# Aligned pairs of PSUM banks, v in even and odd halves, and new orders, in an attention kernel with a maxout layer

## The chip, the cores and the metric

The kernel runs on one core of a Trainium2 chip. The core has a matrix engine (TensorE, PE in the profile), three engines for everything else (VectorE or DVE, ScalarE or ACT, GpSimd or POOL), a queue for transfers (SyncE, SP) and 16 DMA engines. Matrix products land in PSUM, which the kernel uses as eight banks of 512 float32 values per partition; operands lie in SBUF. The engines run beside each other, each through its own instructions in order, and wait for each other by semaphores. The metric is the device time of one execution in microseconds (us), lower is better; the median of several runs is compared.

## The reference

Block-sparse attention with a local window, then a maxout layer with an output projection:

```python
B, H, S, D = q.shape                       # 4, 8, 768, 64
block, window = (32, 16); nb = S // block  # 24 blocks
k_sum = k.reshape(B, H, nb, block, D).max(axis=3)
v_sum = v.reshape(B, H, nb, block, D).mean(axis=3)
scores_l = scale * np.matmul(q, k.transpose(0, 1, 3, 2))
mask_l = np.abs(pos[:, None] - pos[None, :]) < window
scores_s = scale * np.einsum('bhsd,bhnd->bhsn', q, k_sum) + np.log(block)
scores_l_m = np.where(mask_l, scores_l, -1000000000.0)
a = softmax(np.concatenate([scores_l_m, scores_s], axis=-1))
attn = np.matmul(a, np.concatenate([v, v_sum], axis=2))
x = attn.transpose(0, 2, 1, 3).reshape(B * S, H * D)   # 3072 x 512
h1 = x @ w1                                # 512 x 1024
h2 = x @ w2
out = np.maximum(h1, h2) @ w_out           # 1024 x 512
```

Every query sees at most 31 neighbouring keys and the 24 block maxima of its head.

## The kernel before

**Stages.** For each batch b and pair of heads hp (four pairs) `prep` (lines 499 to 569) casts k and q to bf16, transposes them (by TensorE, for six late pairs by a DMA) and builds a key tile `kx`: for every 64 queries 128 columns, namely 64 main keys, 32 neighbours ("tails") and 32 columns for block maxima ("sums"). The maxima come from a reduction on DVE (L546). `cast_v` and `spread_v` (lines 389 to 482) build the value tile `vx` in the same manner. Its original shape is 12 tiles of 64 positions by 8 heads by 66 columns (64 values and ones), with even and odd position tiles alternating in memory. The even tiles are cast from the landed v; odd tiles are copied from them over partitions ("odd v"); block means are made by six matmuls (L459), copied out of PSUM to a tile `sums`, and spread to every position tile ("all sums"). In batch 0 this goes by single pairs of heads, with the block means in tiles of their own (`apart`); in batches 1 to 3 one call does all eight heads.

**Attention.** A batch has three groups (grp) of 256 positions. For each group and two pairs of heads: `scores` (L591) fills one bank per pair of heads; `weigh` takes the exponential of both banks in one ScalarE operation (L603) and multiplies by a 0/1 mask on DVE (L611; in batch 0 the mask is added on TensorE instead, L581); `values` (L641, L645) fills two more banks with weighted values and row sums; DVE inverts the row sums (L657) and scales both banks in one operation (L660) to `xs`, which is transposed to `xt` by a DMA in batches 1 to 3.

**Maxout.** max(h1, h2) is computed as h1 + relu(h2 - h1). The differences w2 - w1 are the tile `wd`, and w1 @ w_out is multiplied out once (`make_w1o`, L732). For each group, `maxout` makes four hidden tiles (L749) with a relu each (L759 on ACT, L761 on DVE), and `out_part` adds x @ (w1 @ w_out) (L777) and relu @ w_out (L784) in one bank, copies it out and stores it.

**What sets the order.** The kernel issues nothing directly. Every step is handed to `plan.op` with its planned duration on each engine that may do it, its buffers and a priority. `Plan.run` (lines 155 to 205) then plays the engines forward in time and always takes the ready step of lowest priority number; the resulting sequence is what each engine gets. Priorities and engines come from two long constants, CFG["prios"] (one number per step) and CFG["engines"] (one letter per step: D, A, P, T, S). Buffers are slots of rings (`Ring`, `Buf`): a step can start only when all slots that it needs are free. The eight PSUM banks are one ring, with limits per kind: 2 for key/query transposes, 4 for scores, 3 for values, 3 for hidden and output (`"mm": 2 + CFG["relu"]`), none for the rest. A wide operation reads its two banks, whichever they are, by one access with a step:

```python
in_=spread(bank_tile[:, pss[0].ap, 0:1], [512 * (pss[1].ap - pss[0].ap), 2], [128, 4], [64, 2], [1, 64]),
...
step = lambda: 512 * (pss[1].ap - pss[0].ap)
```

The semaphores themselves are not written in the kernel: the framework derives them from what each operation reads and writes, in the planned sequence. Small copies of all kinds go through one helper, so that they carry line 492 in the profile; they are told apart by tile and shape.

Of the kernel before, what the change touches and what calls it, by code (L numbers as in the profile page):

```python
# [14 lines left out]
F32 = mybir.dt.float32  # L15
BF16 = mybir.dt.bfloat16
# [10 lines left out]
    woc=600, wdp=30, lk="ADDP", lq="AAPA", lod="DPS", lse="DDD", lsr="DDS", lvc="DPPPDDAPPAPA", ltl="DDPD", ld=500, relu=1, warm=(), cold=12500,  # L27
# [31 lines left out]
""".split()))  # L59
CFG["engines"] = "".join("""  # L60
DPDAADPDDPPDPDPDDADPDDDPPPPSSSDPPPTDDSSSPAPDTDDSSSADPATDDSSSPPPATDASSDATASSPATASSPPTDSSDATDSPSPSASPPTATDDPAPDDDTATDD
PDAADATPTDDADPDDPTPTDDAAPADTTATTDDTATTATTDDTDTTATTDDTDTTATTDDTATTATTDDTATTATTDDTDSSSPSSSASSSASSSDPDADPTADDDDDTPTADPD
PDAATPTDDPPAADTTADTTDDSTTADTTDDSTTADTTDDSDTATADADPAAPTATADDDDDATTADTTDDSTTADTTDDSTTADTTDDSSSSDSSSPSSSASSSPPPPDPTDDDD
PDTPTADAPAAAATPTDDDAAADTTADTTDDSTTADTTDDSTTADTTDDSDSASADPDDDDPSDSADDPPADTTADTTDDSTTADTTDDSTTADTTDDSSSSDSSSDSSSDSSSDP
ADPATDSPDPASDSADDAAPAASASADAPPAATTADTTDDSTTADTTDDSTTADTTDDSDSASDDPAPAPDSASADDPAPDTTADTTDDSTTADTTDDSTTADTTDDSTTATTATT
DTTDTATDTATDTTTDSTTTDSTATDTDTATTTASTTTASTDTATDTATTTASTTTASTATATDTATTTDSTTTASTATATDTDTTTASTTTDSTDTATATDTTTDSTTTASTDTD
TATDTTTASTTTDSTDTATATDTTTASTTTDSTATDTATDTTTASTTTDSTDTDTATATTTDSTTTASTATATDTDTTTASTTTASTATDTATDTTTDSTTTDSTTTDATTTDS
# [4 lines left out]
class Ring:  # L72


    def __init__(self, slots, cap=None):
        self.slots, self.cap = slots, cap or {}
        self.owner = [None] * len(slots)

    def find(self, buf, now):
        ends = [-1 if o is None else o.end() for o in self.owner]  # L80
        if buf.kind in self.cap and self.cap[buf.kind] <= sum(
                o is not None and o.kind == buf.kind and end > now for o, end in zip(self.owner, ends)):
            return None
        return min((s for s, end in enumerate(ends) if end <= now), default=None, key=lambda s: (ends[s], s))


class Buf:
# [11 lines left out]
    def take(self, slot):  # L99
        self.slot, self.ring.owner[slot] = slot, self  # L100

# [107 lines left out]
def kernel(  # L209
# [39 lines left out]
    def bank(buf, n=512, dt=F32):  # L249
        a = bank_tile[:, buf.ap]  # L250
        return (a if dt is F32 else a.bitcast(BF16))[:, 0:n]
# [12 lines left out]
    vxr = Ring(tiles("vx", 2, [128, NT, H, VW], BF16))  # L264
    stg = Ring(tiles("sums", 1, [128, H, VW], BF16))
# [30 lines left out]
    def fixed_parts():  # L296
# [5 lines left out]
        def ones(e, t):  # L302
            on(e).memset(t[:, :, :, D:VW], 1.0)
# [40 lines left out]
        for hs in (slice(0, 4), slice(4, 8)):  # L344
            op("A", {"P": 0.9, "D": 0.85, "A": 0.87}, lambda e, hs=hs: zero(e, by_parity(0)[32:64, 1, :, hs]),
               write=[vx[0], apart_in], prio=0.15, label="gap")
# [29 lines left out]
        op("P", 1.0, lambda e: make_hide(), write=[half[0]], prio=-9, label="hide")  # L376
        for n in range(2):
            op("D", {"D": 0.08, "P": 0.13}, lambda e, n=n: hide_odd(e, 64 * n), read=[half[0]], write=[half[1 + n]],
               prio=-8, port=True, label="hide odd")
        op("D", {"D": 0.08, "P": 0.18}, lambda e: hide_last(e), read=half[:3], write=[half[3]], prio=-8, port=True,  # L380
           label="hide last")
        op("D", {"D": 0.13, "P": 0.2}, lambda e: hide_wrap(e), read=half[3:], write=[hide_in], prio=-8, label="hide wrap")
        op("D", {"D": 0.4, "P": 0.7}, lambda e: on(e).memset(amean[:], 0.0), write=[amean_in], prio=-2, label="amean")
        op("D", {"D": 0.28, "P": 0.45}, lambda e: ones_amean(e), change=[amean_in], prio=0.2, label="amean")
# [28 lines left out]
    def by_parity(b):  # L413
        return vx[b].ap[:].rearrange("p (m w) h c -> p w m h c", w=2)

# [3 lines left out]
    def cast_v(b, hp, engine, prio):  # L419
# [4 lines left out]
            by_parity(b)[:, 0, :, 2 * hp:2 * hp + 2, 0:D].rearrange("p m h d -> p h m d"),  # L424
# [3 lines left out]
    def spread_v(b, h0, h1, prio, engines):  # L428

        n, hs = h1 - h0, slice(h0, h1)  # L430
        src = [mains[b, hp] for hp in range(h0 // 2, h1 // 2)]
        out = [vx[b], *(ready[b, hp] for hp in range(h0 // 2, h1 // 2))]
        took, ps, st = Buf(Ring([None])), Buf(banks, "mm"), Buf(stg)
        tag, whole = f"{b}{h0}", n == H
        s_rows = slice(96, 128)
        if whole:
            fresh = Buf(Ring([None]))
            op("P", 0.2, lambda e: nc.gpsimd.memset(by_parity(b)[s_rows, 0, :, :, D:VW], 1.0),
               read=[mains[b, 0]], write=[vx[b], fresh], prio=prio, label=f"ones {b}")
            src = [*src, fresh]  # L440
# [130 lines left out]
    def scores(b, hp, grp, prio, mask_on):  # L571
# [3 lines left out]
        def view():  # L575
            return bank(ps).rearrange("p (i a w q) -> p i a w q", i=2, a=2, w=2)
# [311 lines left out]
```

## Time and profile before

| what | value |
|---|---|
| median of 3 runs | 194.22 us (194.13 to 196.07) |
| profiled execution | 192.87 us |
| its span, first to last instruction | 191.1 us |
| granted TensorE clock | 1.0 throughout |
| HBM read, written | 25.17 MB, 6.29 MB |
| TensorE weight loads, by the page | 113.2 us |

A row of the page for a group of instructions has the line, engine, operation, what is written from what is read, shapes and count; then the busy time and the mean duration in ns; then the idle time of that engine just before these instructions, and which instruction ended most of it. "PE banks L777 <- ACT pb L603" in the list of waits reads: TensorE, about to run line 777, sat idle until the ScalarE instruction of line 603 ended. Matmuls are pipelined, so the duration of a single one is longer than its share of a running queue.

### The profile page before, as it was taken

The page shows a single profiled execution, that of the slowest core. Times are in us where ns is not written, and L with a number is a line of the kernel's source. Part 1 is how long each engine was busy: PE and PEld are TensorE (multiplying, and loading weights), DVE is VectorE, ACT ScalarE, POOL GpSimd, SP SyncE. Part 2 cuts the span into 40 slices and gives each one's busy share as a digit, 9 for nine tenths or more (in the row PEclk, how much of TensorE's full clock was granted, in tenths as well). Part 3 has the DMA queues.
Part 4 walks back from the last instruction along what each step waited for, and adds up shares of the span by engine and source line. Part 5 has one row for each costly group of instructions (what it writes and reads, how often), then busy time and mean ns, then how long its engine had stood idle before and what let it go on. Part 6 is the DMA issues. An engine that isn't in the chain of part 4 may idle for free.

```text
span 191.1 us, 4050 instructions
## 1 busy us (share of the span) xinstructions
PE 163.3 (85%) x1598; PEld 113.2 (59%) x1598; DVE 117.6 (62%) x236; ACT 104.5 (55%) x143; POOL 57.6 (30%) x86
## 2 busy tenths in 40 slices
PE   0589785999977988899679976999999979998993
PEld 0369785766834654658456643585675547676553
DVE  5988554767974895677676454874778446241212
ACT  8486657765877395475776305756477244223020
POOL 7968689261601210780200002007164000000000
PEclk9999999999999999999999999999999999999999
DMA  6999999999995699349886976987651423134033
GB/s 189 365 261 272 331 370 363 376 365 296 256 245 202 177 230 144 99 70 190 192 230 174 240 189 160 197 209 165 205 135 28 137 42 127 28 95 73 0 110 111
DMA packets 69858, 36.53 MB, mean 191 GB/s; under 512 B 54640, under 2 KB 65872, under 8 KB 69840
## 3 DMA queue, kind: packets, MB, share of 16 engines
q1 hardware_dynamic: 69696, 36.22, 73.8%
q8 instruction: 12, 0.20, 0.5%
q10 hardware_dynamic: 144, 0.07, 0.1%
q14 instruction: 6, 0.05, 0.1%
HBM read 25.17 MB, written 6.29 MB: 165 GB/s over the span
## 4 chain that ended last, share of the span: by engine, by line
PE 69%; DVE 11%; ACT 9%; DMA 6%; issue 2%; SPq 1%; POOL 1%; DVEq 0%; ACTq 0%; POOLq 0%
PE banks L784 19%; PE banks L749 17%; ACT pb L603 9%; PE banks L777 8%; PE banks L591 6%; PE banks L641 6%; DVE vx L492 4%; DVE xs L660 4%; DMA land<-in_q_dram 4%; PE banks L732 4%; PE banks L520 2%; PE banks L459 2%; DMA xt<-xs 2%; PE banks L581 2%; SPq L399 1%
## 5 line engine op out<-in xcount | busy, mean ns | idle before, releaser
L749 PE MATMUL banks<-xt,wd 128*128 128x256 bf16 x384 | 47.0, 272 | 3.0 <-DVE xs L660 1.8
L784 PE MATMUL banks<-wo,g 128*128 128x512 bf16 (+2 forms) x208 | 47.0, 362 | 2.0 <-ACT pb L603 1.1
L749 PEld LDWEIGHTS <-wd 128*128 128x128 bf16 x384 | 36.8, 98 | 11.7 <-issue 3.1
L603 ACT ACTIVATE pb<-banks 128x1024 bf16<-128x1024 f32 x24 | 24.3, 1022 | 26.5 <-PE banks L591 10.0
L784 PEld LDWEIGHTS <-g 128*128 128x128 bf16 x208 | 18.7, 97 | 19.2 <-issue 2.5
L759 ACT ACTIVATE g<-banks 128x512 bf16<-128x512 f32 x24 | 14.3, 598 | 25.0 <-PE banks L749 20.9
L777 PE MATMUL banks<-w1o,xt 128*128 128x512 bf16 (+2 forms) x104 | 24.2, 362 | 2.5 <-ACT pb L603 1.4
L761 DVE TENSOR_SCALAR g<-banks 128x512 bf16<-128x512 f32 x24 | 16.5, 689 | 15.4 <-PE banks L749 12.5
L641 PE MATMUL banks<-vx,pb 128*128 128x65 bf16 (+1 forms) x384 | 19.6, 193 | 3.3 <-ACT pb L603 2.3
L641 PEld LDWEIGHTS <-pb 128*128 128x128 bf16 (+1 forms) x384 | 17.9, 97 | 6.6 <-issue 4.4
L591 PE MATMUL banks<-qx,kx 128*128 128x128 bf16 (+2 forms) x208 | 17.5, 219 | 2.6 <-ACT pb L603 1.7
L591 PEld LDWEIGHTS <-kx 128*128 128x128 bf16 x208 | 14.9, 100 | 7.5 <-issue 3.6
L657 DVE RECIPROCAL inv<-banks 128x8 f32<-128x8 f32 x24 | 5.0, 207 | 22.7 <-PE banks L641 7.3
L660 DVE TENSOR_TENSOR xs<-banks,inv 128x512 bf16<-128x512 f32 x24 | 16.6, 691 | 3.7 <-PE banks L749 2.6
L520 PE MATMUL banks<-ident,kqb 128*128 128x128 f32 x60 | 11.9, 323 | 7.8 <-ACT kqb L492 5.4
L611 DVE TENSOR_TENSOR pb<-pb,mask 128x256 bf16<-128x256 bf16 (+1 forms) x36 | 13.9, 428 | 5.6 <-ACT pb L603 5.6
L492 ACT COPY o<-banks 128x512 f32<-128x512 f32 x13 | 7.6, 586 | 17.3 <-PE banks L784 17.3
L492 DVE COPY o<-banks 128x512 f32<-128x512 f32 (+2 forms) x13 | 7.9, 609 | 13.3 <-PE banks L784 13.1
L777 PEld LDWEIGHTS <-xt 128*128 128x128 bf16 x104 | 9.4, 97 | 11.2 <-issue 1.9
L492 POOL CAST kqb<-land 128x768 bf16<-128x768 f32 x10 | 11.3, 1141 | 14.7 <-ACT vx L492 8.4
L546 DVE TENSOR_REDUCE ks<-kx 128x24 bf16<-128x768 bf16 x16 | 15.1, 945 | 0.2
L492 POOL COPY vx<-vx 32x640 bf16<-32x640 bf16 (+5 forms) x12 | 11.7, 973 | 9.7 <-ACT vx L492 8.2
(85 smaller groups left out, 206.8 us busy)
## 6 DMA issues: line engine op xcount, KB each, us to landing
land<-in_q_dram SPq DMA_DIRECT2D x16, 384.0 KB, 6.6
land<-in_k_dram SPq DMA_DIRECT2D x16, 384.0 KB, 5.3
land<-in_v_dram SPq DMA_DIRECT2D x16, 384.0 KB, 5.8
out_dram<-o SPq DMA_DIRECT2D x19, 256.0 KB, 2.3
land<-in_moe_w_dram SPq DMA_DIRECT2D x8, 512.0 KB, 7.9
land<-in_moe_w_out_dram SPq DMA_DIRECT2D x4, 512.0 KB, 9.7
out_dram<-o SPq DMA_DIRECT2D x4, 224.0 KB, 2.5
xt<-xs SPq DMA_TRANSPOSE x18, 2.5
```

The lines of the kernel that those rows point to most:

```text
L492: {"D": nc.vector.tensor_copy, "A": nc.scalar.copy, "P": nc.gpsimd.tensor_copy}[e](out=o, in_=i)
L520: nc.tensor.transpose(out=bank(ps)[:, 128 * j:128 * j + 128], in_=src.ap[:].bitcast(F32)[:, 128 * j:128 * j + 128], identity=ident32[:])
L546: op("D", 0.95, lambda e: nc.vector.tensor_reduce(out=ks.ap[:, 0:nb], in_=free(kt(), 128, [256, NM], [192, 2], [32, 2], [1, 32]), axis=AX. ...
L591: nc.tensor.matmul(out=view()[:, i // 2, :, i % 2, n0:n1], lhsT=w, rhs=qx[b, hp].ap[:, :, c:c + n1 - n0], start=(mask_on != "T"), stop=(ma ...
L603: op("A", {"A": 1.06}, lambda e: nc.scalar.activation(out=spread(pb.ap[:, :, :, 0:128], [4 * 192, 2], [192, 4], [128, 2], [1, 64]), in_=sp ...
L641: nc.tensor.matmul(out=av(n)[:, u, a, :], lhsT=p[r], rhs=vx[b].ap[r, 4 * grp + 2 * u + par, h, 0:D + 1], start=(par == 0), stop=(b > 0 and ...
L660: op("D", 0.7, lambda e: nc.vector.tensor_tensor(out=x.ap[:].rearrange("p n u a d -> p n (u a) d"), in0=spread(bank_tile[:, pss[0].ap, 0:1 ...
L749: nc.tensor.matmul(out=bank(ps)[:, 256 * s:256 * s + 256], lhsT=wd[n].ap[:, c, 128 * s:128 * s + 128], rhs=x.ap[:, c, :], start=(c == 0), ...
L759: nc.scalar.activation(out=o, in_=i, func=ACT.Relu)
L761: nc.vector.tensor_scalar_max(out=o, in0=i, scalar1=0.0)
L777: nc.tensor.matmul(out=bank(ps, c1 - c0), lhsT=x.ap[:, c, sl], rhs=w1o[c].ap[:, cols], start=(c == 0), stop=False)
L784: nc.tensor.matmul(out=bank(ps, c1 - c0), lhsT=g.ap[:, f, sl], rhs=wo[f // 2].ap[:, f % 2, cols], start=False, stop=(f == FC - 1))
```

## The change

Five edits go together.

1. Rings learn a kind that takes two aligned neighbours (a negative limit). A score group and a value group each take one such pair; at most two pairs of each kind are held. Single buffers prefer a bank whose partner is taken. The limit for hidden and output is 4. `CFG["relu"]` (1 before, which made groups of one) is gone; the relu works on one bank as before.

```diff
+        self.two = {k for k, n in self.cap.items() if n < 0}
...
+        if buf.kind in self.two:
+            ends = [max(ends[s], ends[s + 1]) if s % 2 == 0 else now + 1 for s in range(len(ends))]
+            return min((s for s, end in enumerate(ends) if end <= now), default=None, key=lambda s: (ends[s], s))
+        return min((s for s, end in enumerate(ends) if end <= now), default=None,
+                   key=lambda s: (ends[s ^ 1] <= now, ends[s], s) if self.two else (ends[s], s))
...
-    banks = Ring(list(range(8)), {"kq": 2, "sc": 4, "av": 3, "mm": 2 + CFG["relu"]})
+    banks = Ring(list(range(8)), {"kq": 2, "sc": -2, "av": -2, "mm": 4})
...
-            in_=spread(bank_tile[:, pss[0].ap, 0:1], [512 * (pss[1].ap - pss[0].ap), 2], [128, 4], [64, 2], [1, 64]),
+            in_=spread(bank_tile[:, ps.ap, 0:1], [128, 8], [64, 2], [1, 64]),
...
-            in0=spread(bank_tile[:, pss[0].ap, 0:1], [step(), 2], [D + 1, 4], [1, D]),
+            in0=spread(bank_tile[:, ps.ap, 0:1], [512, 2], [D + 1, 4], [1, D]),
```

2. The value tile has its even and odd position tiles in halves of their own, and within a half the pairs of heads one after the other, so that a copy of several pairs of heads is one long run.

```diff
-    vxr = Ring(tiles("vx", 2, [128, NT, H, VW], BF16))
-    stg = Ring(tiles("sums", 1, [128, H, VW], BF16))
+    vxr = Ring(tiles("vx", 2, [128, 2, NP, NM, 2, VW], BF16))
+    stg = Ring(tiles("sums", 2, [128, H // 2, VW], BF16))
```

3. In batches 1 to 3 `spread_v` is called twice, for two pairs of heads each. A call has one memset of ones, three odd copies (four before, per batch), the block means as six matmuls of 256 columns (512 before), one copy to `sums`, and two spreads (four before, per batch). In these batches the third odd copy comes after the second.

```diff
-        spread_v(b, 0, H, at + 11, (CFG["lod"][b - 1], CFG["lse"][b - 1], CFG["lsr"][b - 1]))
+        for g in (0, 2):
+            spread_v(b, g, g + 2, at + 11 + g, (CFG["lod"][b - 1], CFG["lse"][b - 1], CFG["lsr"][b - 1]))
```

4. In `prep` the tails also wait for the block maxima's reduction, and the spread of the maxima waits for the tails.

```diff
-           read=[kmain, kwrap], write=[kx[b, hp]], prio=prio, label=f"tails k{tag}")
+           read=[kmain, kwrap, ks], write=[kx[b, hp], tailed], prio=prio, label=f"tails k{tag}")
...
-             read=[ks], write=[kx[b, hp]], prio=prio, label=f"sums k{tag}")
+             read=[ks, tailed], write=[kx[b, hp]], prio=prio, label=f"sums k{tag}")
```

5. CFG["prios"] and CFG["engines"] are replaced as a whole (825 steps, 810 before), and a dozen planned durations are altered, such as 1.06 to 1.03 for the exponential, 1.0 to 1.65 for the making of `hide` and 0.49 to 0.51 for the values of batch 0. The durations and priorities act through the sequence alone. By the letters, the four spreads of the block means in batch 1 go from four on DVE to two on DVE, one on ACT and one on POOL; in batches 2 and 3 one odd copy each goes by SP's queue, in place of one spread in batch 3; and the four casts of q in batch 0 go from two on ACT and two on POOL to four on POOL.

More of the change, by code (lines that the diff above doesn't have):

```diff
@@ L77, in __init__ @@
         self.owner = [None] * len(slots)
+        self.two = {k for k, n in self.cap.items() if n < 0}
     def find(self, buf, now):
         ends = [-1 if o is None else o.end() for o in self.owner]
-        if buf.kind in self.cap and self.cap[buf.kind] <= sum(
-                o is not None and o.kind == buf.kind and end > now for o, end in zip(self.owner, ends)):
-            return None
-        return min((s for s, end in enumerate(ends) if end <= now), default=None, key=lambda s: (ends[s], s))
+        if buf.kind in self.cap and abs(self.cap[buf.kind]) <= len({
+                o for o, end in zip(self.owner, ends) if o is not None and o.kind == buf.kind and end > now}):
+            return None
+        if buf.kind in self.two:
[3 more added lines that the diff above has]
+                   key=lambda s: (ends[s ^ 1] <= now, ends[s], s) if self.two else (ends[s], s))
 class Buf:
@@ L100, in take @@
         self.slot, self.ring.owner[slot] = slot, self
+        if self.kind in self.ring.two:
+            self.ring.owner[slot + 1] = self
     @property
@@ L423, in cast_v, with spread_v @@
         copy(engine, {"D": 0.57, "A": 0.84, "P": 0.83}, lambda: (
-            by_parity(b)[:, 0, :, 2 * hp:2 * hp + 2, 0:D].rearrange("p m h d -> p h m d"),
+            vx[b].ap[:, 0, hp, :, :, 0:D].rearrange("p m h d -> p h m d"),
             landed(f, 2, NM * D).rearrange("p h (m d) -> p h m d", d=D)),
              read=[f], write=[vx[b], done, ready[b, hp]], prio=prio, label=f"cast v{b}{hp}")
[L428 to L434, printed above, removed]
+    def spread_v(b, g0, g1, prio, engines):
+        n, late = 2 * (g1 - g0), b > 0
+        hs, gs = slice(2 * g0, 2 * g1), slice(g0, g1)
+        src = [mains[b, hp] for hp in range(g0, g1)]
+        out = [vx[b], *(ready[b, hp] for hp in range(g0, g1))]
+        took, ps = Buf(Ring([None])), Buf(banks, "mm")
+        tag = f"{b}{2 * g0}"
@@ L435, in spread_v @@
         s_rows = slice(96, 128)
-        if whole:
+        if late:
             fresh = Buf(Ring([None]))
-            op("P", 0.2, lambda e: nc.gpsimd.memset(by_parity(b)[s_rows, 0, :, :, D:VW], 1.0),
-               read=[mains[b, 0]], write=[vx[b], fresh], prio=prio, label=f"ones {b}")
+            op("P", {"P": 0.16, "D": 0.14}, lambda e: on(e).memset(vx[b].ap[s_rows, 0, gs].rearrange(
+                "p g m a c -> p (g m a) c")[:, :, D:VW], 1.0),
+               read=src, write=[vx[b], fresh], prio=prio, label=f"ones {b}")
@@ L440, in spread_v, with runs @@
             src = [*src, fresh]
-        def odd(lo, hi, ms, shift):
-            w, ds = by_parity(b), slice(0, VW if whole else D)
-            return (w[lo:hi, 1, ms, hs, ds],
-                    w[lo:hi, 0, slice((ms.start + shift) % NM, (ms.stop + shift - 1) % NM + 1), hs, ds])
-        parts = ((0, NM // 2), (NM // 2, NM)) if whole else ((0, NM),)
-        for i, (lo, hi, ms, shift) in enumerate((
-                *((64, 128, slice(*m), 0) for m in parts), (0, 32, slice(0, NM - 1), 1), (0, 32, slice(NM - 1, NM), 1))):
-            cols = (ms.stop - ms.start) * n * D
-            copy(engines[0], {"D": 0.12 + cols * 0.0003, "P": 0.06 + cols * 0.00095, "A": 0.2 + cols * 0.00083,
-                              **({"S": 1.0 if lo else 0.83 if i == 2 else 0.2} if whole else {})},
-                 lambda lo=lo, hi=hi, ms=ms, shift=shift: odd(lo, hi, ms, shift),
-                 read=src, write=[*out, took], prio=prio, label=f"odd v{tag}{i}")
+        def runs(r, w, m0, m1):
+            t = vx[b].ap[r, w, gs, m0:m1]
+            if late:
+                return t.rearrange("p g m a c -> p g m (a c)")
+            return t.rearrange("p g m a c -> p (g m a) c")[:, :, 0:D]
@@ new lines, in spread_v @@
+        before = []
+        for i, (r, m0, m1, shift) in enumerate((
+                (slice(64, 128), 0, NM, 0), (slice(0, 32), 0, NM - 1, 1), (slice(0, 32), NM - 1, NM, 1 - NM))):
+            cols, done = (m1 - m0) * n * D, Buf(Ring([None]))
+            copy(engines[0], {"D": 0.12 + cols * 0.00032, "P": 0.06 + cols * 0.00095, "A": 0.2 + cols * 0.00083,
+                              **({"S": (1.05, 0.46, 0.12)[i]} if late else {})},
+                 lambda r=r, m0=m0, m1=m1, shift=shift: (runs(r, 1, m0, m1), runs(r, 0, m0 + shift, m1 + shift)),
+                 read=[*src, *before], write=[*out, took, done], prio=prio, label=f"odd v{tag}{i}")
+            before = [done] if i == 1 and late else []
@@ L456, in sums @@
         def sums():
-            w = by_parity(b)
             for m in range(NM):
-                nc.tensor.matmul(out=bank(ps, n * D), lhsT=amean[:, m, :], rhs=w[:, 0, m, hs, 0:D],
+                nc.tensor.matmul(out=bank(ps, n * D), lhsT=amean[:, m, :], rhs=vx[b].ap[:, 0, gs, m, :, 0:D],
                                  start=(m == 0), stop=(m == NM - 1))
@@ L469, in spread_v @@
             return
+        st = Buf(stg)
         copy(engines[1], {"D": 0.12 + n * D * 0.0011, "A": 0.18 + n * D * 0.00083}, lambda: (
-            st.ap[:, hs, 0:D], bank(ps, n * D).rearrange("p (h d) -> p h d", d=D)),
+            st.ap[:, :, 0:D], summed()),
              read=[ps, blocks_in], write=[st], prio=prio, port=False, label=f"sums {tag}")
-        for i, (w, r, ms) in enumerate((w, r, m) for w, r in ((0, s_rows), (1, slice(32, 64))) for m in parts):
-            cols = (ms[1] - ms[0]) * n * VW
-            def aps(w=w, r=r, ms=ms):
-                return (by_parity(b)[r, w, slice(*ms), hs, :],
-                        st.ap[r, hs, :].rearrange("p h d -> p (h d)").rearrange(
-                            "p (o h d) -> p o h d", o=1, d=VW).to_broadcast([32, ms[1] - ms[0], n, VW]))
-            copy(engines[2], {"D": 0.07 + cols * 0.00029, "P": 0.1 + cols * 0.00086,
-                              "A": 0.2 + cols * 0.00083, "S": 0.5}, aps,
-                 read=[st, *([took] if w == 0 else [])], write=out, prio=prio, label=f"all sums {tag}{i}")
+        cols = NM * n * VW
@@ new lines, in spread_v, with aps @@
+        for w, r in ((0, s_rows), (1, slice(32, 64))):
+            def aps(w=w, r=r):
+                a = st.ap[r]
+                return (vx[b].ap[r, w, gs].rearrange("p g m a c -> p g m (a c)"),
+                        spread(a, [2 * VW, g1 - g0], [0, NM], [1, 2 * VW]))
+            copy(engines[2], {"D": 0.12 + cols * 0.00034, "P": 0.1 + cols * 0.00088,
+                              "A": 0.2 + cols * 0.00083}, aps,
+                 read=[st, *([took] if w == 0 else [])], write=out, prio=prio, label=f"all sums {tag}{w}")
@@ L628, in values @@
     def values(b, hp, grp, pb, prio, xt_on="D"):
-        pss, tag = [Buf(banks, "av") for _ in range(2)], f"{b}{hp}{grp}"
+        ps, tag = Buf(banks, "av"), f"{b}{hp}{grp}"
         def av(n):
-            return bank(pss[n])[:, 0:4 * (D + 1)].rearrange("p (u a d) -> p u a d", u=2, a=2)
+            return bank(ps, second=n)[:, 0:4 * (D + 1)].rearrange("p (u a d) -> p u a d", u=2, a=2)
         def mm(n):
@@ L741, in maxout, with hid, relu @@
         x, g = xt[b, grp], Buf(gr)
[L742 to L757 removed]
+        for n in range(4):
+            ps = Buf(banks, "mm")
+            def hid(n=n, ps=ps):
+                for s in range(2):
+                    for c in range(KC):
+                        nc.tensor.matmul(out=bank(ps)[:, 256 * s:256 * s + 256],
+                                         lhsT=wd[n].ap[:, c, 128 * s:128 * s + 128],
+                                         rhs=x.ap[:, c, :], start=(c == 0), stop=(c == KC - 1))
+            op("T", 0.87, lambda e, hid=hid: hid(), read=[x, wd[n]], write=[ps], prio=prio, label=f"hidden {b}{grp}{n}")
+            def relu(e, n=n, ps=ps):
+                o = g.ap[:, 2 * n:2 * n + 2, :].rearrange("p f n -> p (f n)")
                 if e == "A":
[L759 removed]
+                    nc.scalar.activation(out=o, in_=bank(ps), func=ACT.Relu)
                 else:
[L761 to L763 removed]
+                    nc.vector.tensor_scalar_max(out=o, in0=bank(ps), scalar1=0.0)
+            op("A", {"A": 0.6, "D": 0.69}, relu, read=[ps], write=[g], prio=-1, label=f"relu {b}{grp}{n}")
         last = b == B - 1 and grp == NG - 1
@@ L806, in attention @@
             for grp in range(NG):
-                pss = [scores(b, hp, grp, p + 15 + grp, "D") for hp in (2 * half, 2 * half + 1)]
-                pb = weigh(b, 2 * half, grp, pss, p + 15 + grp, "D")
+                ps = Buf(banks, "sc")
+                for hp in (2 * half, 2 * half + 1):
+                    scores(b, hp, grp, ps, p + 15 + grp, "D")
+                pb = weigh(b, 2 * half, grp, ps, p + 15 + grp, "D")
                 values(b, 2 * half, grp, pb, p + 20 + grp, CFG["lx"][b - 1])
@@ L825, in first_attention @@
             for half in range(2):
-                pss = [scores(0, hp, grp, CFG["g0"][grp] + hp, "T") for hp in (2 * half, 2 * half + 1)]
-                pb = weigh(0, 2 * half, grp, pss, CFG["g0"][grp] + 2 * half, "T")
+                ps = Buf(banks, "sc")
+                for hp in (2 * half, 2 * half + 1):
+                    scores(0, hp, grp, ps, CFG["g0"][grp] + hp, "T")
+                pb = weigh(0, 2 * half, grp, ps, CFG["g0"][grp] + 2 * half, "T")
                 values(0, 2 * half, grp, pb, CFG["g1"][grp] + 2 * half, CFG["xt"][2 * grp + half])
```

107 lines of the change are left out of this document (45 added, 62 removed), and 56 rows, old and new, of the table turn.

## The prediction

> **What bounds the kernel now.** I read the page first (busy time, chain), then the busy time by stretch, then who waited for whom on TensorE, then the timeline where TensorE is idle most. The page:
>
> ```profile
> PE 163.3 (85%) x1598; PEld 113.2 (59%) x1598; DVE 117.6 (62%) x236; ACT 104.5 (55%) x143; POOL 57.6 (30%) x86
> PE 69%; DVE 11%; ACT 9%; DMA 6%; issue 2%; SPq 1%; POOL 1%; DVEq 0%; ACTq 0%; POOLq 0%
> ```
>
> TensorE carries the time: 163.3 of 191.1 us busy, 69% of the chain that ended last. The change takes no matmul away, so what it can win is TensorE's idle time, 191.1 - 163.3 = 27.8 us, and its refill after each stop. The busy time by stretch says where that lies (the first figure is the stretch's length, the next TensorE's busy time):
>
> ```profile
> 0.00:12.00 12.00, 4.25 (x16) 2.67 (x16) 9.28 (x26) 7.96 (x12) 9.76 (x30) 1.00 0.91 274
> 12.00:36.00 24.00, 20.46 (x364) 18.90 (x365) 14.94 (x35) 15.73 (x23) 17.44 (x20) 1.00 1.13 332
> ...
> 53.00:60.00 7.00, 4.53 (x26) 2.09 (x25) 4.46 (x13) 5.14 (x6) 0.00 (x0) 1.00 1.03 289
> ...
> 72.00:78.00 6.00, 4.73 (x58) 3.27 (x58) 3.11 (x7) 3.02 (x5) 0.34 (x1) 1.00 0.82 142
> ...
> 90.00:96.00 6.00, 3.64 (x40) 2.64 (x39) 4.44 (x9) 4.36 (x6) 1.18 (x3) 1.00 0.91 193
> ...
> 108.00:120.00 12.00, 8.74 (x77) 4.80 (x75) 5.04 (x13) 4.66 (x7) 1.23 (x1) 1.00 0.77 171
> ...
> 174.00:191.10 17.10, 13.86 (x102) 8.93 (x101) 3.08 (x6) 2.37 (x4) 0.00 (x0) 1.00 0.20 70
> ```
>
> The start (7.75 us idle before 12) waits for loads, and the end (3.24 us after 174) for the last copy and store; no edit is aimed at either. That leaves 27.8 - 7.75 - 3.24 = 16.8 us in between, most of it in short stretches: 2.47 at 53 to 60, 1.27 at 72 to 78, 2.36 at 90 to 96, 3.26 at 108 to 120. No other engine is full there; POOL does nothing at all from 53 to 60. So these are waits, not work. TensorE's waits name them (total us, times, longest):
>
> ```profile
> PE banks L641 <- ACT pb L603: 2.3, 4, 1.1
> PE banks L749 <- DVE xs L660: 1.8, 2, 1.1
> ...
> PE banks L777 <- ACT pb L603: 1.4, 2, 1.1
> PE banks L784 <- ACT pb L603: 1.1, 1, 1.1
> PE banks L459 <- ACT pb L603: 1.1, 1, 1.1
> PE banks L706 <- ACT pb L603: 1.1, 1, 1.1
> PE banks L777 <- DVE xs L660: 1.1, 1, 1.1
> ...
> PE banks L706 <- DVE xs L660: 0.8, 1, 0.8
> PE banks L784 <- DVE xs L660: 0.8, 1, 0.8
> ```
>
> The first row is honest: the value matmuls read pb. The eight others are odd: L777 and L784 (output projection), L749 (hidden layer), L459 (block means) and L706 (weight transposes) use nothing that the exponential L603 or the scaling L660 writes, yet were released by them. Together 1.8+1.4+1.1+1.1+1.1+1.1+0.8+0.8 = 9.2 us in 10 waits, more than half of the 16.8. The timeline shows one such stretch, ACT first and then TensorE:
>
> ```profile
> 53.66 1.02 ACT L603 ACTIVATE pb<-banks 128x1024 bf16<-128x1024 f32 x1 [1.64 <-PE banks L777]
> ...
> 58.38 1.02 ACT L603 ACTIVATE pb<-banks 128x1024 bf16<-128x1024 f32 x1 [1.11 <-PE banks L777]
> ```
> ```profile
> 52.59 1.03 PE L777 MATMUL banks<-w1o,xt 128*128 128x512 bf16 x4
> 54.73 1.02 PE L777 MATMUL banks<-w1o,xt 128*128 128x512 bf16 x4 [1.11 <-ACT pb L603]
> ...
> 59.45 1.02 PE L784 MATMUL banks<-wo,g 128*128 128x512 bf16 x4 [1.11 <-ACT pb L603]
> ```
>
> Each of the two waits for the other: the exponential for a projection matmul that it does not read, the next projection for the exponential. All they share is the PSUM tile `banks`. L603 and L660 read two banks by one access with a step from bank to bank, and the planner hands out any two: banks 0 and 5, say. My reading is that the access counts as touching all that lies between, so that writers of banks 1 to 4 are ordered against it. The trace does not show bank numbers; a bank handed on directly from one to the other would look the same (rival 2).
>
> **The change part by part.**
>
> Aligned pairs. With banks 2i and 2i+1 nothing lies between, so if my reading holds, these waits go. Each also costs refill: four 512-wide matmuls took 1.02 us after a stop, in the rows above, and 0.86 in a running queue:
>
> ```profile
> 100.20 0.86 PE banks L777 x4
> ```
>
> so 10 x 0.16 = 1.6 us more. The upper bound is 9.2 + 1.6 = 10.8 us, the lower nothing. Not all is won: TensorE runs in order, and behind a vanished wait often stands an honest one (the next scores, values or relu result) up to an exponential later. I take half, -5.4 us. That the wide operations get faster themselves I cost at nothing: the exponential reads the same 1024 numbers.
>
> By the Trainium skill ("PSUM — Partial Sum Buffer", the section on bank collisions) two engines have to be kept apart by bank and 32-partition quadrant, and different banks do not collide; by that rule alone the whole 10.8 us would be spare. The rows agree with it only in so far as waits stand where no data passes.
>
> What pairs cost: a score group or value group now needs two neighbouring banks at once, free and aligned, of eight; the limits are two score pairs, two value pairs, 2 key/query banks and 4 of the other kind (3 before). The trace shows no such wait. Its price, where it comes, lies between nothing and one exponential for each of 24 + 24 pairs:
>
> ```profile
> L603 ACT ACTIVATE pb<-banks 128x1024 bf16<-128x1024 f32 x24 | 24.3, 1022 | 26.5 <-PE banks L591 10.0
> ```
>
> I take nothing, since the banks of a pair were filled and freed together before as well, and keep the other end as rival 3.
>
> v in halves and by two head pairs. Odd v copied and block sums spread make a serial stretch on DVE when a batch begins. In batch 1 (first view) POOL's last part stood 8.22 us behind a cast of a head pair that it shares nothing with but the tile; in DVE's own view the four spread copies are one run:
>
> ```profile
> 60.92 0.61 POOL L492 COPY vx<-vx 32x528 bf16<-32x528 bf16 x1 [8.22 <-ACT vx L492]
> ```
> ```profile
> 63.64 0.71 DVE L492 COPY vx<-vx 64x1584 bf16<-64x1584 bf16 x1
> ...
> 65.53 0.97 DVE L492 COPY vx<-vx 32x2640 bf16<-32x2640 bf16 x1
> ...
> 67.11 3.39 DVE L492 COPY vx<-sums 32x1584 bf16<-32x1584 bf16 x4
> ```
>
> That is 5.1 us of DVE (0.71 + 0.97 + 3.39). By the engine letters of the diff the four spreads of batch 1 become two on DVE, one on ACT, one on POOL, and the first two head pairs can go ahead after half of them. In batch 2 three such copies stand in the chain of waits, around the scaling that TensorE waits for, beside the 2.36 us idle of 90 to 96:
>
> ```profile
> 88.33 0.72 DVE vx L492
> ...
> 90.86 0.70 DVE vx L492
> 91.59 0.70 DVE vx L492
> ```
>
> Most of the stretch from 60 to 72 is covered by projection matmuls, so I count little: -1.2 us, bounds 0 and -3.6 (the idle of 72 to 78 and 90 to 96).
>
> Added operations, per later batch: two more odd copies, one more copy of sums, one more memset of ones; the spreads keep their number and size. Fixed costs from the size pairs below: POOL (2646 - 615)/2112 = 0.96 ns an element, so 615 - 528 x 0.96 = 108 ns an operation; for DVE out of PSUM 2 x 426 - 690 = 162 ns.
>
> ```profile
> L492 POOL COPY vx<-vx 32x2640 bf16<-32x2640 bf16 x1 | 2.6, 2646 | 0.5 <-DVE vx L492 0.5
> L492 POOL COPY vx<-vx 32x528 bf16<-32x528 bf16 x2 | 1.2, 615 | 8.3 <-ACT vx L492 8.2
> L492 DVE COPY o<-banks 128x512 f32<-128x512 f32 x10 | 6.9, 690 | 9.4 <-PE banks L784 9.2 <-DMA xt<-xs 0.2
> L492 DVE COPY o<-banks 128x256 f32<-128x256 f32 x1 | 0.4, 426 | 3.5 <-PE banks L784 3.5
> L438 POOL MEMSET vx<- 32x96 bf16 x3 | 0.5, 179 | 0.2
> ```
>
> So 2 x 0.11 + 0.16 + 0.18 = 0.56 us a batch, 1.7 us in all, on three engines none of which is full: +0.2 on the path; 1.7 if that cover is gone. The block means become twelve matmuls of 256 in place of six of 512, the same columns. Two odd parts go by SP's queue in place of one spread. The one now took 2.5 us to land; they are loads' neighbours on the queue, and the first scaled results go there too. I count 0, at worst 2 x 2.5 = 5.
>
> ```profile
> vx<-sums SPq DMA_DIRECT2D x1, 99.0 KB, 2.5
> ```
>
> Keys: the tails now come after the maximum, the block maxima after the tails, 16 times one maximum of latency at most. Behind a waiting tail on ACT stand exponentials, on POOL casts of the next head pairs; behind both, scores.
>
> ```profile
> L546 DVE TENSOR_REDUCE ks<-kx 128x24 bf16<-128x768 bf16 x16 | 15.1, 945 | 0.2
> ```
>
> Between 0 and 16 x 0.95 = 15 us; where a tail is DVE's own its queue orders it anyway, and keys are placed well ahead of their scores, so I take +0.4, near the lower end.
>
> Orders anew. Every priority and many engine letters are new (DVE loses work to ACT and POOL); casts of q in batch 0 all go to POOL. I cannot cost this from rows; its bounds are the other 16.8 - 9.2 = 7.6 us of idle won, or as much lost. I take 0.
>
> Sum: 192.87 us (the profiled execution, 1.8 above its span of 191.1) - 5.4 - 1.2 + 0.2 + 0.4 = 186.9. The median of the runs, 194.22, is 1.35 above that execution; so 188.2 us is forecast for the median.
>
> "Judge a full TensorE by weight-load time, not matmul busy time" is the rule of the Trainium skill ("Perfetto Trace Analysis", Identifying the Most-Contended Engine). With 59% for weight loads beside 85% the page would see room below 163.3 us too. The trace agrees as far as the 0.16 us of refill go.
>
> **The rivals.**
>
> 1. Forecast: false waits half gone. Chance 0.55; with a quarter to four fifths of the 10.8 us won it gives 190.9 to 185.0.
>
> 2. The waits were honest: the freed bank is the one that the projection takes next. Then pairs change nothing: 194.22 - 1.2 + 0.6 = 193.6, the same within noise. For it: eight banks for limits that add up to 12, so banks are handed on at once. Against it: at 53.66 the exponential too waited for a projection, and it only reads. Chance 0.14.
>
> 3. Slower: pairs starve. The place is the scores: TensorE's queue stops at a score group until two aligned neighbours are free, and matmuls behind it stop too. At 1.02 us a time, the net gain of 6.0 us is eaten up by 6 waits, and with 8 the kernel is slower by 1%; if half of the 24 score pairs wait, 188.2 + 12.2 = 200.4. For it: one more bank for hidden and output, two more tied up by scaled values than a limit of three single ones. Against it: single banks are now handed out from broken pairs first. Chance 0.17.
>
> 4. All goes: 10.8 us of waits, and v's 3.6: 194.22 - 14.4 + 0.6 = 180.4. Chance 0.14.
>
> **The numbers.** This kernel tells 1% (1.9 us) from no change. Faster by more: nearly all of the forecast (0.53), all of rival 4, little of rival 2: 0.68. Same: rival 2 and edges, 0.15. Slower: 0.17. The range from 182.5 to 195.5 us leaves out half of rival 4 and most of rival 3.
>
> **What would show it.** Right: rows of TensorE released by L603 or L660 at L777, L784, L749, L459 and L706 are gone or under 3 us together; no exponential is released by a projection matmul; TensorE's idle time is near 21 us. Step by step: POOL's 8.22 us wait gone and DVE's run of four spreads cut to two; the tails behind the maxima without new rows at the scores. Wrong: the same rows with the same sums (rival 2), or score and value matmuls released by exponentials or scalings for over 6 us together (rival 3), or a start later than 12 us because of POOL's casts.

## The result, and the profile after

The changed kernel takes 176.61 us (median of 4 runs, 175.97 to 177.68) where the kernel before takes 194.78 (4 runs, 194.13 to 196.07): 0.9065 of it, 95% interval 0.8989 to 0.9141. Forecast were 188.2 us and a range from 182.5 to 195.5; the direction was right, the gain three times as large as forecast. The profiled execution took 177.22 us, its span 175.4.

The page of the changed kernel, first busy time, then the chain (lines have moved: L604 scores, L615 exponential, L653 values, L668 inversion, L671 scaling, L759 hidden layer, L786 and L793 output, L468 block means, L505 the copy helper):

```profile
PE 159.9 (91%) x1597; PEld 115.4 (66%) x1616; DVE 116.1 (66%) x227; ACT 110.7 (63%) x161; POOL 61.5 (35%) x89
...
PE 70%; DMA 9%; SPq 5%; ACT 5%; DVE 4%; issue 3%; POOL 1%; ACTq 0%; DVEq 0%
```

TensorE's idle time fell from 27.8 to 175.4 - 159.9 = 15.5 us, and its busy time from 163.3 by 3.4 us. Together that is the 15.7 us of span. The columns multiplied are the same (the block means of a later batch go as twelve matmuls of 256 columns in place of six of 512, and the trace lacks 19 of the 1616 matmul records), so the 3.4 us are put down to fewer stops and less refill; a run below with exactly the old matmuls shows the same 159.9. The clock granted to TensorE was 0.99 to 1.0 in nearly all executions, but about 0.98 in those of the kernel before on the second of three chips below (198.16 us) and in some on the third, and 0.968 to 0.983 in those of the kernel with banks four apart, so that times are set beside the 194.78 and 176.61 us above where a ratio would mislead. ACT's and DVE's part in the chain, 9% and 11% before, is 5% and 4%.

The busy time by stretch (length of the stretch, then TensorE's busy time):

```profile
0.00:12.00 12.00, 4.23 (x18) 2.67 (x18) 9.00 (x21) 9.17 (x17) 8.16 (x32) 1.00 0.92 265
12.00:36.00 24.00, 22.48 (x376) 20.37 (x376) 19.56 (x42) 18.19 (x25) 14.34 (x14) 1.00 1.09 335
...
53.00:60.00 7.00, 6.91 (x55) 4.18 (x54) 6.78 (x10) 5.89 (x9) 4.53 (x6) 1.00 1.22 273
...
108.00:120.00 12.00, 11.50 (x96) 7.75 (x97) 6.48 (x13) 9.10 (x15) 1.47 (x3) 1.00 0.98 220
...
156.00:175.40 19.40, 15.95 (x107) 9.40 (x106) 2.79 (x5) 3.21 (x6) 0.00 (x0) 0.99 0.24 82
```

Start and end are as idle as before (12 - 4.23 = 7.77 and 19.4 - 15.95 = 3.45 us). What lies between fell from 16.8 to 15.5 - 7.77 - 3.45 = 4.3 us. What TensorE still waited for, as the list of waits has it:

```profile
PE banks L533 <- ACT kqb L505: 7.1, 2, 5.4
PE banks L533 <- DVE sums L505: 1.0, 1, 1.0
PE banks L533 <- POOL kqb L505: 0.8, 2, 0.6
PE banks L686 <- issue: 0.4, 1, 0.4
PE banks L533 <- DVE qx L505: 0.4, 1, 0.4
PE banks L468 <- POOL vx L505: 0.4, 1, 0.4
PE banks L786 <- ACT g L768: 0.4, 1, 0.4
PE banks L604 <- DVE xs L671: 0.3, 1, 0.3
```

The largest is that of the first transposes, which wait for the first loads and casts. Of the eight odd rows that the prediction added up to 9.2 us none is left.

### The profile page after: what moved, and what is told of

Same layout as the page of the kernel before. It is cut to its first block, busy times and chain, and to the rows that moved or that the text cites. A ratio compares the mean times of both kernels' runs of the same rounds, so it can differ in the third digit from the quotient of the medians.

```text
span 175.4 us, 4098 instructions
## 1 busy us (share of the span) xinstructions
PE 159.9 (91%) x1597; PEld 115.4 (66%) x1616; DVE 116.1 (66%) x227; ACT 110.7 (63%) x161; POOL 61.5 (35%) x89
## 4 chain that ended last, share of the span: by engine, by line
PE 70%; DMA 9%; SPq 5%; ACT 5%; DVE 4%; issue 3%; POOL 1%; ACTq 0%; DVEq 0%
PE banks L793 19%; PE banks L759 18%; PE banks L786 8%; PE banks L653 6%; PE banks L604 5%; DMA land<-in_v_dram 5%; SPq L408 4%; PE banks L743 3%; DMA land<-in_k_dram 3%; PE banks L533 2%; PE banks L468 2%; PE banks L594 2%; PE banks L657 2%; DMA kt<-kqb 2%; DVE kx L505 1%
## 5 line engine op out<-in xcount | busy, mean ns | idle before, releaser
L793 PE MATMUL banks<-wo,g 128*128 128x512 bf16 (+2 forms) x198 | 46.2, 362 | 0.5
L759 PE MATMUL banks<-xt,wd 128*128 128x256 bf16 x384 | 46.7, 273 | 0.0
L759 PEld LDWEIGHTS <-wd 128*128 128x128 bf16 x384 | 37.0, 98 | 7.1
L615 ACT ACTIVATE pb<-banks 128x1024 bf16<-128x1024 f32 x24 | 24.0, 1023 | 7.1 <-PE banks L604 6.7
L793 PEld LDWEIGHTS <-g 128*128 128x128 bf16 x208 | 18.5, 98 | 14.0
L768 ACT ACTIVATE g<-banks 128x512 bf16<-128x512 f32 x27 | 15.9, 597 | 18.6 <-PE banks L759 18.5
L770 DVE TENSOR_SCALAR g<-banks 128x512 bf16<-128x512 f32 x21 | 14.3, 688 | 19.4 <-PE banks L759 19.4
L786 PE MATMUL banks<-w1o,xt 128*128 128x512 bf16 (+2 forms) x97 | 23.8, 361 | 0.8 <-ACT g L768 0.4
L505 ACT COPY o<-banks 128x512 f32<-128x512 f32 (+1 forms) x16 | 9.0, 564 | 18.2 <-PE banks L793 18.1
L653 PEld LDWEIGHTS <-pb 128*128 128x128 bf16 (+1 forms) x384 | 17.8, 97 | 4.0 <-ACT pb L615 0.2
L653 PE MATMUL banks<-vx,pb 128*128 128x65 bf16 (+1 forms) x384 | 19.4, 193 | 0.0
L505 POOL CAST kqb<-land 128x768 bf16<-128x768 f32 x13 | 14.6, 1132 | 10.6 <-DMA land<-in_k_dram 4.5
L604 PE MATMUL banks<-qx,kx 128*128 128x128 bf16 (+2 forms) x208 | 17.8, 220 | 0.4 <-DVE xs L671 0.3
L604 PEld LDWEIGHTS <-kx 128*128 128x128 bf16 x208 | 14.9, 100 | 3.9 <-issue 0.7
L623 DVE TENSOR_TENSOR pb<-pb,mask 128x256 bf16<-128x256 bf16 (+1 forms) x36 | 16.4, 497 | 1.6 <-ACT pb L615 1.5
L533 PEld LDWEIGHTS banks<-ident,kqb 128*128 128x128 f32 x60 | 7.9, 162 | 12.9 <-POOL amean L382 5.4
L671 DVE TENSOR_TENSOR xs<-banks,inv 128x512 bf16<-128x512 f32 x24 | 16.1, 682 | 0.4
L505 POOL COPY vx<-vx 32x1320 bf16<-32x1320 bf16 (+3 forms) x9 | 10.4, 1152 | 17.0 <-DVE vx L505 10.6
L505 DVE COPY o<-banks 128x512 f32<-128x512 f32 (+2 forms) x10 | 6.2, 622 | 14.4 <-PE banks L793 14.3
L786 PEld LDWEIGHTS <-xt 128*128 128x128 bf16 x104 | 9.6, 98 | 8.8 <-issue 0.7
(86 smaller groups left out, 213.4 us busy)
```

The source lines that it names most:

```text
L505: {"D": nc.vector.tensor_copy, "A": nc.scalar.copy, "P": nc.gpsimd.tensor_copy}[e](out=o, in_=i)
L533: nc.tensor.transpose(out=bank(ps)[:, 128 * j:128 * j + 128], in_=src.ap[:].bitcast(F32)[:, 128 * j:128 * j + 128], identity=ident32[:])
L604: nc.tensor.matmul(out=view()[:, i // 2, :, i % 2, n0:n1], lhsT=w, rhs=qx[b, hp].ap[:, :, c:c + n1 - n0], start=(mask_on != "T"), stop=(ma ...
L615: op("A", {"A": 1.03}, lambda e: nc.scalar.activation(out=spread(pb.ap[:, :, :, 0:128], [192, 8], [128, 2], [1, 64]), in_=spread(bank_tile ...
L623: nc.vector.tensor_tensor(out=o, in0=o, in1=spread(mask[:, 2 * i:2 * i + 2], [0, o.shape[1]], [64, 2], [1, 64]), op=ALU.mult)
L653: nc.tensor.matmul(out=av(n)[:, u, a, :], lhsT=p[r], rhs=vx[b].ap[r, par, hp + n, 2 * grp + u, a, 0:D + 1], start=(par == 0), stop=(b > 0 ...
```

## The experiments

Two things were new at once, the places of the banks and the whole order of the work, and v besides. Theory W: the gain is the false waits' going; an access to two banks is ordered against everything that lies between them. Theory O: the new orders bring it. Theory V: the separate halves of v do. Different runs met different chips, on which the kernel before took 195.69, 198.16 and 197.09 us in the median; a ratio is to the kernel before on the run's own chip.

**Pairs four banks apart, everything else as changed.** The planner, the order and every operation stay; only the banks' numbers change, so that three foreign banks lie inside each pair. The exponential and both DVE operations get the new step.

```diff
-    banks = Ring(list(range(8)), {"kq": 2, "sc": -2, "av": -2, "mm": 4})
+    banks = Ring([0, 4, 1, 5, 2, 6, 3, 7], {"kq": 2, "sc": -2, "av": -2, "mm": 4})
...
-        a = bank_tile[:, buf.ap + second]
+        a = bank_tile[:, buf.ap + 4 * second]
```

> The changed kernel with its order and all operations kept; only the banks are renumbered, so that the two banks of a pair lie four apart (0 and 4, 1 and 5, ...). Theory W (false waits: a wide access is ordered against everything between its two banks): projection, hidden and block-mean matmuls are released by exponentials and scalings again, and 8 to 15 us come back, 185 to 192 us. Theory O (the new orders bring the gain): nothing is waited for that was not before, 175 to 179 us.

Its median is 213.4 us, 1.0816 of the kernel before (interval 1.0712 to 1.0921): slower than both, and far more than expected. Part of this is the clock. But in the profiled execution the clock was low only between 20 and 60 us (0.81, then 0.85), and outside that stretch TensorE was idle for 32.5 us, against 14.9 in the changed kernel. The exponential itself takes 1023 ns in both, so the distance of the banks costs waits and does not slow the access. TensorE's waits in it:

```profile
PE banks L653 <- ACT pb L615: 6.7, 5, 4.0
PE banks L793 <- ACT pb L615: 4.1, 3, 2.0
...
PE banks L717 <- ACT pb L615: 1.2, 1, 1.2
PE banks L468 <- ACT pb L615: 1.1, 1, 1.1
PE banks L786 <- ACT pb L615: 1.1, 1, 1.1
```

The output projection (L793, L786), weight transposes (L717) and block means (L468) are released by exponentials again. Nothing about data, order or engines differs from the changed kernel, and each bank passes from user to user in the same sequence as there, so neither theory O nor an honest handing-on of banks (the prediction's rival 2) can account for it.

**The kernel before, wide operations split.** Order, banks and layout of before; exponential, inversion and scaling are each made by two instructions that touch one bank.

```diff
+        def exps(e):
+            for n in range(2):
+                nc.scalar.activation(
+                    out=spread(pb.ap[:, n, :, 0:128], [192, 4], [128, 2], [1, 64]),
+                    in_=spread(bank_tile[:, pss[n].ap, 0:1], [128, 4], [64, 2], [1, 64]),
+                    func=ACT.Exp, scale=scale)
```

> The kernel before with its order and banks kept; the exponential, the inversion and the scaling are each made by two instructions of one bank, so that no access reaches over other banks. That adds about 0.2 us to each of 24 exponentials and 0.1 to each of 48 DVE operations. Theory W: the eight rows of odd waits go and the kernel falls to 180 to 187 us in spite of the added instructions. Theory O: 194 to 199 us.

175.51 us, 0.9002 of the kernel before (0.893 to 0.9074). This is less time than theory W was expected to give (180 to 187 us), and as much as the whole change brings, with the old order, the old v and 72 instructions more on ACT and DVE. Its page, its stretches at the start and at the end, and all of TensorE's waits:

```profile
PE 159.9 (93%) x1598; PEld 113.2 (66%) x1598; DVE 120.9 (70%) x284; ACT 105.2 (61%) x167; POOL 57.3 (33%) x86
```
```profile
0.00:12.00 12.00, 4.31 (x15) 2.50 (x15) 9.28 (x26) 7.77 (x12) 8.99 (x29) 1.00 0.89 270
...
156.00:172.80 16.80, 13.70 (x102) 8.82 (x100) 3.08 (x6) 2.37 (x4) 0.00 (x0) 1.00 0.18 62
```
```profile
PE banks L520 <- ACT kqb L492: 5.4, 1, 5.4
PE banks L520 <- POOL kqb L492: 2.3, 2, 1.3
PE banks L520 <- DVE kqb L492: 0.7, 1, 0.7
PE banks L591 <- ACT qx L492: 0.5, 1, 0.5
PE banks L756 <- DMA xt<-xs: 0.5, 1, 0.5
```

Idle are 172.8 - 159.9 = 12.9 us, of which 7.69 at the start and 3.10 at the end. The middle, 16.8 us before, has 2.1 left: the old order had hardly any stall of its own. The matmuls are the old 1598, and their busy time is 3.4 us shorter.

**The same split in the changed kernel**, as control:

> The changed kernel with the wide operations made by two instructions each, as control for what the split itself costs where nothing is gained by it. Theories W and O both: 0 to 4 us more than the changed kernel, 176.6 to 181 us; it is to be added to what the split of the kernel before wins.

176.31 and 181.27 us in two executions, the second at a clock of 0.99. The first is level with the 176.61 of the changed kernel: where no bank lies between, splitting shows no gain, as far as one execution tells.

**The changed kernel with v as it was laid out before**, even and odd tiles alternating, order kept:

```diff
-    vxr = Ring(tiles("vx", 2, [128, 2, NP, NM, 2, VW], BF16))
+    vxr = Ring(tiles("vx", 2, [128, NT, H, VW], BF16))
```

> The changed kernel with its order kept; the value tile has the layout of before, even and odd tiles alternating. Theory W: the halves are worth little by themselves, 177 to 181 us. Theory V (the separate halves free the copies of v from waiting for each other): 184 us or more, with waits of POOL and DVE at vx for ACT's casts.

177.5 us, 0.9085 (0.9027 to 0.9143): no difference from the changed kernel that can be measured. Theory V falls. This tests where v lies; the spread by two pairs of heads stayed in.

**One kind of wide operation split at a time**, in the kernel before:

> The kernel before with its order kept, only the exponential made by two instructions of one bank; inversion and scaling still reach over the banks between. If the two kinds of wide access cost about alike (the odd rows of TensorE's waits had 4.7 us by exponentials and 4.5 by scalings), about half of the 20 us goes: 183 to 189 us. If the exponential carries it alone, 175 to 180.

> The same with only inversion and scaling made by two instructions each, the exponential as it was. Alike: 183 to 189 us. If the exponential carries it alone: 192 us or more.

Exponential alone: 184.59 us, 0.9305 (0.9255 to 0.9354). Inversion and scaling alone: 186.56 us, 0.9426 (0.9377 to 0.9476). These ratios flatter both, since the kernel before ran at the lower clock beside them. Beside its 194.78 us the gains are 10.2 and 8.2 us, together 18.4, and splitting both at once gained 19.3: the two kinds share the cost about equally, and their gains about add up. In the first, TensorE's odd rows by scalings remain and those by exponentials are gone:

```profile
PE banks L752 <- DVE xs L663: 2.0, 2, 1.1
PE banks L780 <- DVE xs L663: 1.1, 1, 1.1
PE banks L709 <- DVE xs L663: 0.9, 1, 0.9
...
PE banks L787 <- DVE xs L663: 0.8, 1, 0.8
```

In the second it is the other way round: the output projection, block means and weight transposes wait for exponentials (1.4, 1.3, 1.1 and 1.1 us), and no row by a scaling is left.

**Split only where banks lie between.** In the kernel before, the wide form stays where the two banks happen to be neighbours, aligned or not:

```diff
+            if abs(pss[1].ap - pss[0].ap) == 1:
+                nc.scalar.activation(
...
+                return
+            for n in range(2):
```

> The kernel before with its order and banks kept; wide operations stay whole where their two banks are neighbours, aligned or not, and are split only where banks lie between. If only what lies between counts, this is as good as splitting all, 173 to 176.5 us, with a third fewer added instructions. If neighbours have to be aligned, it keeps some of the waits: over 178 us.

176.51 us (175.24 to 178.42), about level with the 175.51 of the full split; the ratio, 0.8884 (0.8822 to 0.8947), owes about 2% to the lower clock of the kernel before (198.16 against 194.78 us). The groups of its exponentials, from a second run of it (below), show how many had neighbours anyway, 9 of 24 (30 halves make the other 15):

```profile
L611 ACT ACTIVATE pb<-banks 128x512 bf16<-128x512 f32 x30 | 16.2, 604 | 5.8 <-DVE xs L683 3.3 <-PE banks L591 2.5
...
L605 ACT ACTIVATE pb<-banks 128x1024 bf16<-128x1024 f32 x9 | 9.1, 1022 | 6.4 <-PE banks L591 6.4
```

By the planner of this kernel, played forward, five of these nine pairs are neighbours that are not aligned (banks 1 and 2, say), and the time is no worse for them. So alignment is not what counts, only what lies between.

**Pairs two banks apart**, one foreign bank between, in the changed kernel:

> The changed kernel with its order kept and the banks renumbered so that the two of a pair lie two apart, one foreign bank between instead of three. If the cost goes with what lies between, it stands between the changed kernel and the one with four apart: 182 to 200 us. If only the form of the access (a step that is not one bank) costs, as much as with four apart: 207 us or more.

181.86 us (181.34 to 182.43), just below what was expected. The ratio, 0.9177 (0.9137 to 0.9216), is again flattered by the clock of the kernel before; in time it is 2 to 3% above the changed kernel, which took 176.61 us above and 178.32 on the third chip below, and their executions do not overlap. Some of the odd rows are back, small ones:

```profile
ACT pb L615 <- PE banks L759: 1.2, 1, 1.2
DVE xs L671 <- PE banks L793: 1.1, 2, 0.8
...
PE banks L793 <- ACT pb L615: 0.2, 1, 0.2
```

So one bank between costs a little and three cost much. That speaks against the form of the access as the cause: a step of two banks has the same form as a step of four.

**The two best side by side**, on one chip, five rounds:

> The changed kernel itself, beside the next run on the same chip, for a direct comparison: about 0.906 of the kernel before.

> The kernel before with its own order, layout and spreads of v, its wide operations split only where banks lie between them. If the new orders, the halves of v and the spread by two pairs are worth something beside the pairs, it is slower than the changed kernel by over 1%; if the removal of false waits is all, it is level with it, within 1%, or ahead by the pairs' tighter limits.

Changed kernel 178.32 us (177.13 to 179.12), 0.909 (0.9015 to 0.9166); kernel before with split where needed 175.74 us (175.36 to 176.59), 0.897 (0.8912 to 0.9029). All six runs of the second lie below all six of the first. So the old order and the old v, freed of false waits, do better than the whole change by some 2.6 us. The two kernels differ in the orders, the halves of v, its spread by two head pairs, the order of tails and maxima, and the tighter limits that pairs set to the planner; the experiments do not divide the 2.6 us among them. A gain by one of these may be hidden under a loss by another.

**Without the two constants.** The planner then goes by the priorities and engines written at the calls:

> The kernel before without its two constants: the planner goes by the priorities and engines written at the calls. Longer than with them: 195 to 215 us. It is the base for the next run.

> The same without the two constants, all wide operations split. If false waits hurt any order alike, it is shorter than the run before it by 15 to 25 us; if they hurt only a sequence that was fitted closely to planned durations, by less than 10.

203.8 and 207.6 us without the split, 181.8 and 183.8 with it; the first of each, at the same clock of 0.99, are 22 us apart. On two executions each, false waits hurt a plain order about as much as the finely fitted one.

Not run: the pairs alone on the old constants, since the planner with these comes to a point at which no step finds its banks free; and the order of tails and maxima by itself.

## Why the prediction was wrong

**The mechanism was right.** It read the eight odd rows of TensorE as false waits from accesses that reach over banks, and named what would show it: rows gone (all are), no exponential released by a projection matmul (none is; the only matmuls that it waits for are the scores', 6.7 us in a row below), TensorE's idle time near 21 us (it is 15.5, so here the size was off).

**The step that failed** is the size of the first term, aligned pairs: "I take half, -5.4 us", with 10.8 us as the upper bound. By itself, in the old order, the removal is worth 10.0% of 195.69, or 19.5 us, beyond the bound. Two things were wrong in that term.

First, the bound. It counted eight rows in which TensorE itself was released by a wide operation, and left the rest out or took it as honest. Even of TensorE's own rows five more, 3.2 us by exponentials, scalings and an inversion at scores, values and the hidden layer, are gone after the split. And the wide operations waited falsely as well, and made honest successors late. The list of waits of the kernel before has these rows, which the prediction did not add up:

```profile
DVE inv L657 <- PE banks L784: 6.6, 3, 3.6
ACT pb L603 <- PE banks L784: 6.5, 1, 6.5
...
ACT pb L603 <- PE banks L777: 4.4, 4, 1.6
...
ACT pb L603 <- PE banks L706: 1.8, 1, 1.8
...
DVE inv L657 <- PE banks L777: 1.4, 1, 1.4
```

The exponential reads only scores, the inversion only values, yet they stood 6.5 + 4.4 + 1.8 = 12.7 and 6.6 + 1.4 = 8.0 us for projections and weight transposes. For the exponential and the inversion the changed kernel's list has

```profile
ACT pb L615 <- PE banks L604: 6.7, 9, 1.4
...
DVE inv L668 <- PE banks L653: 4.0, 6, 1.7
```

and no row for a projection or a weight transpose. A late exponential means late values, late scaled values and a late hidden layer: rows such as "L641 <- ACT pb L603: 2.3", called honest in the prediction, vanished with the others. The bound that would have held was the whole middle, 16.8 us, and the 3.4 us of busy time that went with it.

Second, the half. It assumed an honest wait behind each false one. The split of the kernel before shows 2.1 us of 16.8 left, so seven eighths went. The refill was under-counted too: 1.6 us by ten stops, 3.4 us by the busy time, presumably since stops too short for the list empty the queue as well; that was not tested.

**Rival 4** ("all goes", 180.4 us, given 0.14) was the nearest. It came out short because its 10.8 us carried the same bound; its 3.6 us for v show in no run.

**Rival 2** (honest waits) and **rival 3** (starving pairs) fell. In the changed kernel the only wait of matmuls listed at the scores is one of 0.3 us, and none stands at the values. (Its "two more" banks tied up by scaled values are one more by the limits, two pairs against three single banks.)

**v, -1.2 us**: the halves brought nothing, by the old layout run in the changed order; the spread by two pairs has no run of its own. The serial stretch on DVE was broken up as told, with two of batch 1's spreads left there, but a long wait of POOL was not removed. It stands later, at another copy:

```profile
71.12 3.19 POOL L505 COPY vx<-vx 64x1584 bf16<-64x1584 bf16 x2 [7.11 <-DVE vx L505]
```

TensorE's list has a single row by POOL's copies, of 0.4 us.

**Added operations, +0.2, and keys, +0.4**: no run separates them. **Orders, 0**: no gain shows; in the direct comparison they are part of the 2.6 us by which the changed kernel is behind. **POOL's casts of q** did not delay the start: TensorE was busy 4.23 us of the first 12, 4.25 before.

## What to carry to other kernels

Where an engine is released by an instruction that shares no data with it, ask what storage the two share and how far the access of the wide one reaches. If it steps over other buffers, place its parts side by side, or split it where they are not: two instructions of 602 ns in place of one of 1022 cost ACT 24 x 0.18 = 4.4 us here, and TensorE, which sets the time, won far more. When such a wait is priced, add up the waits in both directions and count what follows a late instruction; the bound is the idle time of the stretch, not the rows with the telling name.

## What the runs showed of the hardware that was not expected

A copy in SBUF on DVE took nearly four times as long beside one on POOL. In the changed kernel the odd copy of 32 x 1320 took 0.48 us at 133.0 us of the span, with POOL idle, and 1.81 us at 57.78. POOL's and DVE's timelines there:

```profile
57.27 1.96 POOL L505 COPY vx<-vx 64x1584 bf16<-64x1584 bf16 x1 [0.67 <-DVE vx L445]
```
```profile
57.78 1.81 DVE L505 COPY vx<-vx 32x1320 bf16<-32x1320 bf16 x1
```

DVE's copy ends at 59.59, 0.36 us after POOL's at 59.23: it seems to have stood until POOL was through. The Trainium skill ("SBUF — State Buffer", the section on the two separate sides) says that POOL shares one port pair with DVE, and that of an operation on POOL and one on DVE that uses this pair too the first to start holds it for its whole instruction, while the other blocks; the trace agrees with that here, though it does not show which ports a copy uses. Over the kernel the two DVE copies of 64 x 1584 averaged 1674 ns, 706 ns before. That copies of v on POOL slow those on DVE may be part of why the new orders win nothing; this was not tested.
